# A state-space scan followed by a two-layer network on one Trainium2 core: the chunk's x tile in two halves, the first loads in another order, fewer filler matmuls and decode passes before the network starts, and eleven network cells in place of nine

## The chip, the core and the metric

The kernel runs on one core of a Trainium2 (trn2) chip. The metric is the device time of one execution, in microseconds (us); lower is better. Engines are named as in the profile: PE is TensorE, with PEld its weight loads, DVE is VectorE, ACT is ScalarE, POOL is GpSimd, and SP is the queue from which nearly all DMA transfers are issued.

## The reference

A scan with a decaying state runs per batch and head, and a two-layer network with a leaky ReLU runs on its result. The shapes are 4 batches, 8 heads, 768 positions, head width 32 and state width 16; the network has width 256, inner width 2048, and 3072 tokens.

```python
for c in range(nc):                                    # chunks of a sequence
    cum = np.cumsum(la, axis=-1)                       # la = log(clip(a))
    L = np.exp(cum[:, :, :, None] - cum[:, :, None, :]) * causal
    CB = np.einsum('bhin,bhjn->bhij', Cc, Bc)
    y_intra = np.einsum('bhij,bhjd->bhid', CB * L, xc)
    y_inter = np.einsum('bhin,bhnd->bhid', Cc, state) * np.exp(cum)[:, :, :, None]
    y[:, :, sl] = y_intra + y_inter
    Bx = np.einsum('bhjn,bhjd->bhjnd', Bc, xc) * np.exp(cum[:, :, -1:] - cum)[..., None, None]
    state = np.exp(np.sum(la, axis=-1))[:, :, None, None] * state + np.sum(Bx, axis=2)
...
h = x @ w_in                                           # x: y of all heads, 3072 x 256
g = np.maximum(0.01 * h, h)
return (g @ w_out).astype(np.float32)
```

The two weight matrices arrive as 64-bit floats, the rest as 32-bit floats.

## The kernel before

**The scan.** The kernel cuts the sequence into 8 chunks of 96 positions. One *unit* u is one chunk c of one batch b (u = 4c + b), so there are 32 units of 96 tokens. For a unit, PE computes the scores of its heads into PSUM tiles `sc` (`scores`, L288) and the exponents of its decay into a PSUM tile `pd` (`decay_pe`, L234); ACT takes the exponential into `lt` (L242); DVE multiplies the scores into `lt` (L293, two instructions a unit). PE then multiplies `lt` with the chunk's x tile `xs` (`unit_products`, L305), and `xs` with `bn` for the state that goes to the next chunk (L314). ACT copies that state to `stage` (L336), POOL copies it from there into the last 16 rows of the next chunk's `xs` (L339, four instructions a unit), ACT rounds the result to `xh` (L341), and DVE stores what the rounding lost in `xl` (L344). The names `bc`, `bn` and `xs` are the inputs of a chunk, loaded by `fetch_bc`, `fetch_bn` and `fetch_x`. POOL multiplies the decay into `bn` (`state_decay`, L269).

**The lead-in.** Units 0 to 15 run before the network, in one loop (L579 and after). Iteration u issues `scores(u + 1)`, the products of unit u, the decay of unit u + 2, then `xl` of unit u, and then some weight-decode passes. The second argument of `scores` is a number of dummy matmuls of a zero tile (`keep_warm`, L104) that PE runs first: two for u = 0 and 1, and one for every later u, 17 in all. `score_tile` has two buffers and `free_tile` (`pd`) has two, so the products of unit u + 1 may start only when `xh` and `xl` of unit u have been read out of their tile.

**The weights.** The inner width is cut into 16 blocks f of 128. The 64-bit weights of a block (`raw`, `fetch_w`) are turned into a 32-bit value and then into two rounded halves, `wh` and `wl`. It takes an `Abs` on ACT (`decode_abs`, L390) and, in this order on DVE, the passes hold (L395), shift (L401), rest of block f - 1 (L428, which makes `wl`), sign (L408) and low (L415), and a cast on ACT between low and rest (`decode_high`, L421, which makes `wh`). `decode(n)` runs the next n DVE passes. The lead-in runs 17 of the 79; the table `PASSES` gives how many follow in each step of the network.

**The network.** The 3072 tokens form six tiles t of 512. One *step* is a pair (t, f): `ffn_in` issues six matmuls of 128 x 128 by 512 columns into `hp` (L486; in each half of the input the order is `xh` by `wh`, `xh` by `wl`, `xl` by `wh`), ACT makes `gh` (L493) and the activated `hp` (L496), DVE makes `gl` (L499), and three steps later `ffn_out` issues six matmuls into the accumulators `op` (L510). The table `CELLS` gives the order of the steps: a cell (t, lo, hi) is tile t with the blocks lo to hi - 1. At the end of a cell the accumulators are copied out or added to what an earlier cell of the tile left (L527, L531, L533). Units 16 to 31 run in pairs within the network, after the steps in the table `PAIR` (`pair_block`).

**What sets the order.** Each engine runs its instructions in the order in which this code issues them; nothing reorders them afterwards. SP's queue is issued in that order too. In the lead-in's code the first loads are: `la`, `bc` and `xs` of chunk 0; then, after the split sums, `parts_d`, `bn` of chunk 0, weight block 0, the rows `dr` and `dl` for the decay of units 2 to 5 (`decay_rows_of`), `bc`, `bn` and `xs` of chunk 1, block 1 and `xs` of chunk 2.

## Time and profile before

| | |
|---|---|
| median of the runs | 327.06 us (327.05 to 327.64, 3 runs) |
| the profiled execution | 326.36 us, of which the traced span is 324.7 us |
| PE busy over the span | 316.9 us (98%), 2439 matmuls |
| DVE, ACT, POOL busy | 160.3, 167.4 and 80.5 us |
| DMA moved | 27.86 MB, 86 GB/s on average |
| first matmul of the network | 40.76 us after the span's start |

A row of a timeline gives the start in us from the span's start, the duration in us, the engine, the line, the operation, the tile written and the tiles read, the shapes, and how many like instructions were merged into the row (x2). In brackets stand the idle time of the engine before it and what ended that. The word "issue" means that the engine waited for nothing that the profile shows. A DMA row on SPq is the time of issuing, not of the transfer. Busy times of PE overlap, since matmuls are pipelined: starts tell more than durations there.

### The profile page before, as it was taken

The page shows a single profiled execution, that of the slowest core. Times are in us where ns is not written, and L with a number is a line of the kernel's source. Part 1 is how long each engine was busy: PE and PEld are TensorE (multiplying, and loading weights), DVE is VectorE, ACT ScalarE, POOL GpSimd, SP SyncE. Part 2 cuts the span into 40 slices and gives each one's busy share as a digit, 9 for nine tenths or more (in the row PEclk, how much of TensorE's full clock was granted, in tenths as well). Part 3 has the DMA queues.
Part 4 walks back from the last instruction along what each step waited for, and adds up shares of the span by engine and source line. Part 5 has one row for each costly group of instructions (what it writes and reads, how often), then busy time and mean ns, then how long its engine had stood idle before and what let it go on. Part 6 is the DMA issues. An engine that isn't in the chain of part 4 may idle for free.

```text
span 324.7 us, 6255 instructions
## 1 busy us (share of the span) xinstructions
PE 316.9 (98%) x2439; PEld 250.4 (77%) x2440; DVE 160.3 (49%) x305; ACT 167.4 (52%) x334; POOL 80.5 (25%) x164
## 2 busy tenths in 40 slices
PE   8889999999999999999999999999999999999995
PEld 4456587888788877887788888888878788888883
DVE  5679978967688543524434342525252312322221
ACT  5567776674756545353454545453544444444431
POOL 3667820000010243454034543434210000000000
PEclk9999999999999999999999999999999999999999
DMA  5998032342891001602311090202010000100001
GB/s 159 311 312 249 30 118 73 129 131 78 281 297 32 1 0 67 203 9 74 107 23 65 0 280 27 87 2 86 2 65 2 0 0 2 63 3 0 3 0 65
DMA packets 10616, 27.86 MB, mean 86 GB/s; under 512 B 2170, under 2 KB 2650, under 8 KB 10586
## 3 DMA queue, kind: packets, MB, share of 16 engines
q1 hardware_dynamic: 10442, 27.33, 26.9%
q8 instruction: 19, 0.31, 0.4%
q10 hardware_dynamic: 144, 0.13, 0.1%
q14 instruction: 11, 0.09, 0.1%
HBM read 24.14 MB, written 3.32 MB: 85 GB/s over the span
## 4 chain that ended last, share of the span: by engine, by line
PE 95%; DMA 2%; DVE 1%; issue 1%; ACT 0%; SPq 0%; ACTq 0%
PE op L510 41%; PE hp L486 39%; PE sc L288 2%; PE pd L305 2%; PE sc L365 2%; PE sc L305 2%; PE pd L234 2%; PE sc L104 1%; DMA dl<-parts_d 1%; PE sc L486 1%; PE pd L314 1%; DMA parts_d<-parts 0%; PE sc L314 0%; PE pd L208 0%; DVE lt L293 0%
## 5 line engine op out<-in xcount | busy, mean ns | idle before, releaser
L499 DVE TENSOR_TENSOR gl<-hp,gh 128x512 fp32r<-128x512 f32 x94 | 65.0, 691 | 143.7 <-ACT hp L496 143.3
L493 ACT ACTIVATE gh<-hp 128x512 fp32r<-128x512 f32 x94 | 56.1, 597 | 110.6 <-PE hp L486 110.6
L510 PE MATMUL op<-gh,wh 128*128 128x512 f32 x192 | 76.3, 397 | 0.0
L510 PE MATMUL op<-gh,wl 128*128 128x512 f32 x192 | 74.8, 390 | 0.0
L510 PE MATMUL op<-gl,wh 128*128 128x512 f32 x192 | 74.8, 389 | 0.0
L486 PE MATMUL hp<-xh,wh 128*128 128x512 f32 x188 | 73.3, 390 | 0.0
L486 PE MATMUL hp<-xl,wh 128*128 128x512 f32 x188 | 73.2, 389 | 0.0
L486 PE MATMUL hp<-xh,wl 128*128 128x512 f32 x188 | 73.1, 389 | 0.0
L496 ACT ACTIVATE hp<-hp 128x512 f32<-128x512 f32 x94 | 55.7, 593 | 0.0
L510 PEld LDWEIGHTS op<-gh,wh 128*128 128x128 f32 x192 | 36.0, 188 | 10.5 <-issue 2.3
L510 PEld LDWEIGHTS op<-gl,wh 128*128 128x128 f32 x192 | 36.0, 188 | 7.6
L510 PEld LDWEIGHTS op<-gh,wl 128*128 128x128 f32 x192 | 36.1, 188 | 7.1
L339 POOL COPY xs<-stage 16x64 f32<-16x64 f32 x112 | 31.3, 280 | 39.7 <-ACT stage L336 29.6
L486 PEld LDWEIGHTS hp<-xh,wl 128*128 128x128 f32 x188 | 35.3, 188 | 7.4
L486 PEld LDWEIGHTS hp<-xh,wh 128*128 128x128 f32 x188 | 35.3, 188 | 7.4
L486 PEld LDWEIGHTS hp<-xl,wh 128*128 128x128 f32 x188 | 35.3, 188 | 7.3
L254 POOL TENSOR_TENSOR lt<-lt,ccol 112x768 f32<-112x768 f32 x16 | 23.5, 1469 | 50.5 <-DMA lt<-crow_d 49.4
L263 POOL TENSOR_SCALAR_AFFINE_SELECT lt<-lt 96x768 f32<-96x768 f32 x16 | 14.0, 875 | 59.5 <-ACT lt L262 59.5
L293 DVE TENSOR_TENSOR lt<-sc,lt 112x384 f32<-112x384 f32 x32 | 16.3, 549 | 3.1 <-ACT lt L242 1.9
L374 DVE TENSOR_TENSOR lt<-sc,lt 112x384 f32<-112x384 f32 x32 | 15.6, 549 | 0.5
L262 ACT ACTIVATE lt<-lt 112x768 f32<-112x768 f32 x16 | 13.4, 839 | 4.1 <-POOL lt L254 4.1
L242 ACT ACTIVATE lt<-pd 112x768 f32<-112x768 f32 x16 | 13.1, 816 | 2.1 <-PE pd L215 2.1
(89 smaller groups left out, 242.4 us busy)
## 6 DMA issues: line engine op xcount, KB each, us to landing
raw<-w_l SPq DMA_DIRECT2D x16, 512.0 KB, 3.4
lt<-crow_d SPq DMA_DIRECT2D x16, 336.0 KB, 4.7
bc<-bc_l SPq DMA_DIRECT2D x8, 608.0 KB, 5.8
xs<-x_l SPq DMA_DIRECT2D x8, 384.0 KB, 9.4
out_l<-ob SPq DMA_DIRECT2D x11, 256.0 KB, 2.8
bn<-bn_l SPq DMA_DIRECT2D x8, 231.0 KB, 5.7
out_l<-obh ACTq DMA_DIRECT2D x1, 128.0 KB
out_l<-obh SPq DMA_DIRECT2D x1, 128.0 KB, 1.8
```

The lines of the kernel that those rows point to most:

```text
L242: nc.scalar.activation(lt.rearrange("p (g h) i -> p g (h i)", g=2), space[:QE, :, :4 * Q], AF.Exp)
L254: nc.gpsimd.tensor_tensor(out=lts[u], in0=lts[u], in1=ccol[:, u * NH:(u + 1) * NH].unsqueeze(2).to_broadcast([QE, NH, Q]), op=ALU.subtract,)
L262: nc.scalar.activation(lt, lt, AF.Exp)
L263: nc.gpsimd.affine_select(out=lt[:Q], in_=lt[:Q], pattern=[[0, NH], [1, Q]], compare_op=ALU.is_ge, fill=0.0, base=0, channel_multiplier=-1,)
L293: nc.vector.tensor_tensor(out=heads, in0=sc[:QE, :, :2 * Q], in1=heads, op=ALU.mult)
L339: nc.gpsimd.tensor_copy(to[:, :, hh], stage[hh * D:hh * D + N])
L374: nc.vector.tensor_tensor(out=heads, in0=spaces[half][:QE, :, 2 * Q * e:2 * Q * (e + 1)], in1=heads, op=ALU.mult,)
L486: nc.tensor.matmul(hp, lhsT=w_half[half][:, f, k * 128:(k + 1) * 128], rhs=x[t][:, k, :], start=(n == 0), stop=(n == 5),)
L493: nc.scalar.activation(ghs[s], hp, AF.Prelu, alpha=0.01)
L496: nc.scalar.activation(hps[s], hps[s], AF.Prelu, alpha=0.01)
L499: nc.vector.tensor_tensor(out=gls[s], in0=hps.pop(s), in1=ghs[s], op=ALU.subtract)
L510: nc.tensor.matmul(op, lhsT=w_half[half][:, f, DM + m * 128:DM + (m + 1) * 128], rhs=x, start=(first and i == 0), stop=(last and i == 2),)
```

## The change

The x tile of a chunk becomes two tiles of two batches each, loaded by two transfers of 2 KB a row. `bn` of chunk 0 is loaded right behind the x of chunk 0, weight block 0 behind `bc` of chunk 1, and x of chunk 1 ahead of `bn` of chunk 1. The lead-in runs one dummy for u = 2 and 3 and none from u = 4 on (6 in all), and 12 decode passes, with the first two of them and the first `Abs` one unit later. `CELLS` has eleven cells, with tiles 0, 1 and 2 visited in turn, and `PASSES` and `PAIR` change with it.

```diff
 CELLS = (
-    (0, 0, 3), (1, 0, 6), (2, 0, 6), (0, 3, 16), (1, 6, 16), (2, 6, 16), (3, 0, 16), (4, 0, 16),
-    (5, 0, 16),
+    (0, 0, 2), (1, 0, 4), (2, 0, 6), (0, 2, 10), (1, 4, 12), (2, 6, 16), (0, 10, 16), (1, 12, 16),
+    (3, 0, 16), (4, 0, 16), (5, 0, 16),
...
-PAIR = {16: 28, 18: 33, 20: 38, 22: 45, 24: 51, 26: 56, 28: 61, 30: 68}
+PAIR = {16: 29, 18: 34, 20: 38, 22: 44, 24: 51, 26: 56, 28: 61, 30: 68}
...
-PASSES = (1, 1, 2, 2, 4, 1, 4, 4, 3, 3, 3, 0, 3, 3, 3, 3, 2, 0) + (3,) * 7
+PASSES = (2, 2, 2, 4, 1, 2, 2, 2, 1, 3, 2, 3, 3, 3, 1, 3, 3, 2) + (3, 3, 3, 3, 0) + (3,) * 6
...
     def alloc_x(c):
-        xss[c] = pxs.tile([QE, NB, DM], F32, name="xs")
+        for g in range(2):
+            xss[c, g] = pxs.tile([QE, NB // 2, DM], F32, name="xs")
...
     fetch_x(0)
+    fetch_bn(0)
...
         nc.sync.dma_start(parts_d, parts)
-        fetch_bn(0)
-        fetch_w(0)
         decay_rows_of(DIRECT, SLOTS)
         fetch_bc(1)
+        fetch_w(0)
+        fetch_x(1)
         fetch_bn(1)
-        fetch_x(1)
         fetch_w(1)
...
-        decode_abs(0)
         for u in range(PE_DECAY):
             if u + 1 < PE_DECAY:
-                scores(u + 1, 2 if u < 2 else 1)
+                scores(u + 1, (2, 2, 1, 1)[u] if u < 4 else 0)
...
-            if u == 0:
+            if u == 1:
+                decode_abs(0)
                 decode(2)
-            elif u != 3:
+            elif u in (2, 3) or u % 2:
                 decode(1)
-            if u == 2:
+            if u == 1:
                 state_decay(1)
...
         settle()
-        decode(1)
+        decode(2)
```

How the order moves is shown at three places. Line numbers of the changed kernel are 6 or 7 higher. The first place is SP's queue from the x of chunk 0 to the x of chunk 2, before:

```order
L96 DMA xs<-x_l 96x1024
L561 DMA parts_d<-parts 128x288
L90 DMA bn<-bn_l 112x528
L82 DMA raw<-w_l 128x1024
L224 DMA dr<-parts_d 3x32x96
L227 DMA dl<-parts_d 24x4x96
L86 DMA bc<-bc_l 128x1216
L90 DMA bn<-bn_l 112x528
L96 DMA xs<-x_l 96x1024
L82 DMA raw<-w_l 128x1024
L96 DMA xs<-x_l 96x1024
```

and now:

```order
L100 DMA xs<-x_l 96x512 x2
L90 DMA bn<-bn_l 112x528
L568 DMA parts_d<-parts 128x288
L231 DMA dr<-parts_d 3x32x96
L234 DMA dl<-parts_d 24x4x96
L86 DMA bc<-bc_l 128x1216
L82 DMA raw<-w_l 128x1024
L100 DMA xs<-x_l 96x512 x2
L90 DMA bn<-bn_l 112x528
L82 DMA raw<-w_l 128x1024
L100 DMA xs<-x_l 96x512 x2
```

The first `bn` and the first `raw` no longer stand between `parts_d` and the `dr` and `dl` that are read from it.

The second place is DVE in the lead-in, from `xl` of unit 0 over the multiply of unit 2 (the first L293) to that of unit 3 (`w_202` before and `w_292` now are weight block 0), before:

```order
L344 TENSOR_TENSOR xl<-pd,xh 128x2x96
L395 TENSOR_SCALAR w_202<-w_202 128x512
L401 TENSOR_SCALAR w_202<-w_202 128x512
L293 TENSOR_TENSOR lt<-sc,lt 112x384 x2
L344 TENSOR_TENSOR xl<-pd,xh 128x2x96
L408 SCALAR_TENSOR_TENSOR w_202<-raw,w_202 128x512
L293 TENSOR_TENSOR lt<-sc,lt 112x384 x2
```

and now:

```order
L351 TENSOR_TENSOR xl<-pd,xh 128x2x96
L300 TENSOR_TENSOR lt<-sc,lt 112x384 x2
L351 TENSOR_TENSOR xl<-pd,xh 128x2x96
L402 TENSOR_SCALAR w_292<-w_292 128x512
L408 TENSOR_SCALAR w_292<-w_292 128x512
L300 TENSOR_TENSOR lt<-sc,lt 112x384 x2
L351 TENSOR_TENSOR xl<-pd,xh 128x2x96
```

Hold and shift of block 0 now stand between `xl` of unit 1 and the multiply of unit 3; their `Abs` stands on ACT behind the exponential of unit 3.

The third place is DVE where the network starts, from the last multiply of the lead-in to the second `gl` (before, `w_813` is block 3 and `w_600` block 2; now `w_764` is block 2 and `w_380` block 1), before:

```order
L293 TENSOR_TENSOR lt<-sc,lt 112x384 x2
L344 TENSOR_TENSOR xl<-pd,xh 128x2x96
L395 TENSOR_SCALAR w_813<-w_813 128x512
L344 TENSOR_TENSOR xl<-pd,xh 128x2x96
L401 TENSOR_SCALAR w_813<-w_813 128x512
L428 TENSOR_TENSOR wl<-w_600,wh 128x512
L499 TENSOR_TENSOR gl<-hp,gh 128x512
L408 SCALAR_TENSOR_TENSOR w_813<-raw,w_813 128x512
L499 TENSOR_TENSOR gl<-hp,gh 128x512
```

and now:

```order
L300 TENSOR_TENSOR lt<-sc,lt 112x384 x2
L351 TENSOR_TENSOR xl<-pd,xh 128x2x96 x2
L402 TENSOR_SCALAR w_764<-w_764 128x512
L408 TENSOR_SCALAR w_764<-w_764 128x512
L435 TENSOR_TENSOR wl<-w_380,wh 128x512
L506 TENSOR_TENSOR gl<-hp,gh 128x512
L415 SCALAR_TENSOR_TENSOR w_764<-raw,w_764 128x512
L422 SCALAR_TENSOR_TENSOR w_764<-raw,w_764 128x512
L506 TENSOR_TENSOR gl<-hp,gh 128x512
```

The last `wl` that DVE makes ahead of the first `gl` was that of block 2 and is now that of block 1, and the pass ahead of the last `xl` is now behind it.

More of the change, by code (lines that the diff above doesn't have):

```diff
@@ L63, in scan_ffn @@
     pbc = ctx.enter_context(tc.tile_pool(name="pbc", bufs=2))
-    pxs = ctx.enter_context(tc.tile_pool(name="pxs", bufs=3))
+    pxs = ctx.enter_context(tc.tile_pool(name="pxs", bufs=6))
     plt = ctx.enter_context(tc.tile_pool(name="plt", bufs=4))
@@ L92, in alloc_x @@
     def alloc_x(c):
-        xss[c] = pxs.tile([QE, NB, DM], F32, name="xs")
+        for g in range(2):
+            xss[c, g] = pxs.tile([QE, NB // 2, DM], F32, name="xs")
     def fetch_x(c, eng=nc.sync):
-        eng.dma_start(xss[c][:Q].rearrange("p b c -> p (b c)"), x_l[c])
+        for g in range(2):
+            n = NB // 2 * DM
+            eng.dma_start(
+                xss[c, g][:Q].rearrange("p b c -> p (b c)"), x_l[c][:, g * n:(g + 1) * n]
+            )
     idle = const.tile([128, 512], BF16, name="idle")
@@ L300, in unit_products @@
         kk = QE if c else Q
-        mt, xs = lts[u], xss[c][:, b]
+        mt, xs = lts[u], xss[c, b // 2][:, b % 2]
         for g in range(2):
@@ L336, in unit_halves @@
             nc.scalar.copy(stage, space[:, :, off + Q:off + Q + D])
-            to = xss[c + 1][Q:QE, b].rearrange("n (g h d) -> n g h d", g=2, d=D)
+            to = xss[c + 1, b // 2][Q:QE, b % 2].rearrange("n (g h d) -> n g h d", g=2, d=D)
             for hh in range(4):
```

## Prediction

> **What bounds the kernel now.** I read the page first: its span, PE's busy share and the granted clock.
>
> ```profile
> span 324.7 us, 6255 instructions
> PE 316.9 (98%) x2439; PEld 250.4 (77%) x2440; DVE 160.3 (49%) x305; ACT 167.4 (52%) x334; POOL 80.5 (25%) x164
> PEclk9999999999999999999999999999999999999999
> ```
>
> 98% hides two different stages. A view by windows shows the network's start:
>
> ```profile
> 40.00:56.00 16.00, 15.99 (x98) 12.82 (x99) 12.84 (x25) 11.43 (x24) 2.58 (x8) 1.00 0.29 99
> ```
>
> PE is busy for 15.99 of 16 us: in the network PE is the bound, and no edit here removes any of its 1152 matmuls. Time can be won only ahead of the first network matmul (T), and lost wherever PE comes to wait. In the lead-in I read the timeline of unit 8, a plain one:
>
> ```profile
> 27.17 0.36 DVE L344 TENSOR_TENSOR xl<-pd,xh 128x192 fp32r<-128x192 f32 x1 [0.18 <-ACT xh L341]
> 27.45 0.68 DVE L408 SCALAR_TENSOR_TENSOR w<-raw,w 128x512 uint32<-128x512 uint32 x1
> 27.71 0.32 PEld L305 LDWEIGHTS pd<-lt,xs 112*32 112x32 f32 x16 [0.24 <-DVE xl L344]
> 28.04 1.01 DVE L293 TENSOR_TENSOR lt<-sc,lt 112x384 f32<-112x384 f32 x2
> 28.31 0.53 PE L234 MATMUL pd<-dr,dl 123*112 123x384 bf16 x2
> 28.53 0.21 ACT L336 COPY stage<-pd 128x64 f32<-128x64 f32 x1 [0.64 <-POOL xs L339]
> 28.68 0.38 PE L104 MATMUL sc<-idle 128*128 128x512 bf16 x1
> 28.99 0.71 PE L288 MATMUL sc<-bc 32*112 32x192 f32 x8
> 29.00 0.36 DVE L344 TENSOR_TENSOR xl<-pd,xh 128x192 fp32r<-128x192 f32 x1
> 29.62 0.54 PE L305 MATMUL pd<-lt,xs 112*32 112x96 f32 x16
> ...
> 21.92 0.54 PE L305 MATMUL pd<-lt,xs 112*32 112x96 f32 x16
> 38.92 0.54 PE L305 MATMUL pd<-lt,xs 112*32 112x96 f32 x16
> ```
>
> Three loops run at nearly the same pace. PE from products to products takes 29.62 - 27.71 = 1.91, of which the dummy takes 28.99 - 28.68 = 0.31. DVE from `xl` to `xl` takes 1.83 with a decode pass in it. The third goes around: products to `stage` 0.82, `stage` to `xl` 0.47, `xl` itself 0.36, and a wake-up of about 0.05 (below): 1.70. The last two rows are the products of units 5 and 14: nine units in 17.00 us, 1.89 each.
>
> **The change part by part.** *The start.* The rows of units 0 to 2, with the quiet round trip of one small transfer:
>
> ```profile
> 7.92 0.32 SPq L227 DMA_DIRECT2D dl<-parts_d  x1
> 9.59 1.06 POOL L269 TENSOR_TENSOR bn<-bn,erev 112x512 f32<-112x512 f32 x1 [4.24 <-DMA bn<-bn_l]
> 10.70 0.33 PE L314 MATMUL pd<-xs,bn 96*32 96x32 f32 x16 [0.27 <-POOL bn L269]
> 11.43 0.66 ACT L390 ACTIVATE w<-raw 128x512 f32<-128x512 f32 x1 [1.57 <-DMA raw<-w_l]
> 11.70 0.53 PE L234 MATMUL pd<-dr,dl 123*112 123x384 bf16 x2 [0.66 <-DMA dl<-parts_d]
> 12.71 0.43 DVE L395 TENSOR_SCALAR w<-w 128x512 f32<-128x512 f32 x1
> 13.53 1.02 DVE L293 TENSOR_TENSOR lt<-sc,lt 112x384 f32<-112x384 f32 x2
> 14.28 0.81 ACT L242 ACTIVATE lt<-pd 112x768 f32<-112x768 f32 x1
> 15.32 1.02 DVE L293 TENSOR_TENSOR lt<-sc,lt 112x384 f32<-112x384 f32 x2
> ...
> parts_d<-parts SPq DMA_DIRECT2D x1, 72.0 KB, 1.6
> ```
>
> POOL ends at 10.65 and PE starts at 10.70: the wake-up of 0.05. With `bn` loaded early the wait of 0.27 goes. With nothing but `bc` behind it in the queue, `dl` issued at 7.92 lands by about 7.92 + 1.6 = 9.5, so the 0.66 goes too: 0.93 earlier. It is then given back. `Abs` of block 0 now stands behind the exponential of unit 3, and hold and shift behind it stand ahead of the scores of unit 3 on DVE. That exponential starts at 14.28 - 0.93 = 13.35 and ends at 14.16; `Abs` 0.66 gives 14.82; hold to the next multiply takes 13.53 - 12.71 = 0.82, so the multiply of unit 3 comes at 15.64 against 15.32. Instructions of one engine overlap a little (in unit 8 the pass at 27.45 starts 0.08 before the `xl` ahead of it has ended), and the start to start of this chain is shorter for that, so I take 0; the ends are 0.3 later and 0.9 earlier.
>
> *The stall at unit 4.* PE stops in the middle of one unit's products, with no semaphore:
>
> ```profile
> 18.77 0.44 PE L305 MATMUL pd<-lt,xs 112*32 112x96 f32 x9
> 20.29 0.37 PE L305 MATMUL pd<-lt,xs 112*32 112x96 f32 x7 [1.08 <-issue]
> ...
> q1 hardware_dynamic: 518, 1.36, 101.2%
> q8 instruction: 1, 0.02, 1.8%
> ```
>
> The last two rows are the DMA view of 17 to 21 us: all engines are full of loads, and one block of program code goes through in that stretch. I read the 1.08 us as PE waiting for code behind the loads. The loads stay the same but for one early `bn`, and by the zero above PE comes here at about the same time. The ends are 0 and 1.08 earlier; in between I take 0.5.
>
> [...]
>
> *Units 5 to 14.* Without dummies PE's loop falls to 1.60; the loop through ACT and DVE stays at 1.70; DVE's stays at 1.83 where a two-input pass is left (units 9, 11 and 13). Nine units: 6 x 1.70 + 3 x 1.83 = 15.7, so 1.3 are won. More code blocks come in this stretch, and a faster PE reaches them sooner: I take 1.2. The ends are 0 (code) and 9 x 0.29 = 2.6 (PE alone). *Edits at nothing.* The two x tiles make two DMA issues of one, some 0.4 of SP's time each; behind them in the queue stand loads for units that come 4 us and more later, and no row above waits for x. If that cover fails, a late x shows as PE waiting for DMA at unit 4. `state_decay` of chunk 1 moves ahead of unit 2's state copies on POOL; if `bn` of chunk 1 is late, those copies queue behind it, and the next to wait are units 6 and 7, four units (4 x 1.70 = 6.8 us) later.
>
> The first matmul of the network thus comes 1.7 earlier.
>
> *The network's start.* Here are the rows around T = 40.76:
>
> ```profile
> 40.76 0.50 PE L486 MATMUL hp<-xh,wh 128*128 128x512 f32 x1
> 41.48 0.36 DVE L344 TENSOR_TENSOR xl<-pd,xh 128x192 fp32r<-128x192 f32 x1 [0.56 <-ACT xh L341]
> 41.75 0.41 DVE L401 TENSOR_SCALAR w<-w 128x512 uint32<-128x512 uint32 x1
> 42.08 0.72 DVE L428 TENSOR_TENSOR wl<-w,wh 128x512 fp32r<-128x512 f32 x1
> 42.48 0.39 PE L486 MATMUL hp<-xh,wl 128*128 128x512 f32 x1
> 43.57 0.69 DVE L499 TENSOR_TENSOR gl<-hp,gh 128x512 fp32r<-128x512 f32 x1 [0.77 <-ACT hp L496]
> 43.81 0.60 ACT L493 ACTIVATE gh<-hp 128x512 fp32r<-128x512 f32 x1 [0.27 <-PE hp L486]
> 45.38 0.58 ACT L493 ACTIVATE gh<-sc 128x512 fp32r<-128x512 f32 x1
> 47.92 0.39 PE L486 MATMUL hp<-xh,wl 128*128 128x512 f32 x1
> 55.34 0.19 PEld L510 LDWEIGHTS op<-gh,wh 128*128 128x128 f32 x1 [0.43 <-DVE ob L533]
> ```
>
> Step 1 is block 1, and its second matmul (42.48, T + 1.72) needs `wl` of block 1. Before, that was made in the lead-in; now it is the third pass behind the last `xl`. That `xl` starts at T + 0.72; hold follows after 0.27, shift after 0.43 (12.71's duration), `wl` after 0.33, and it lasts 0.72: T + 2.47. PE waits 0.75 there. Step 4 is block 2. ACT starts `gh` of step 1 at T + 3.05 + 0.75 = 3.8; the six passes gh, hp, `Abs`, the cast of `wh`, gh, hp follow at (45.38 - 43.81) / 3 = 0.52 and end at about 7.0; `gl` of step 2 takes 0.69, and `wl` of block 2 ends 0.72 later, at T + 8.4. PE needs it at 47.92, T + 7.16 + 0.75 = 7.9: another 0.5. Step 5 needs block 3, whose low, hold, shift and `wl` all stand behind `gl` of step 3, which stands behind `wl` of block 2: I estimate 0.45 by the same durations, and 0.25 for the accumulator of the two-block cell, whose copy on DVE ends behind them. Sum: 1.95. The ends are 0.75 (the later ones hidden) and 3.0. Before, none of these waits is there: from 42.48 to 47.92 PE starts 24 matmuls at an even 0.227 us.
>
> *Two more cells.* The last row is such a boundary: PE's weight loads stood still for 0.43. Two more cost 0 (if other work hides them) to 0.9; I take half, 0.4. The tables `PAIR` and the later `PASSES` move work between steps in which DVE has room: a step is 12 matmuls, 12 x 0.227 = 2.72 us, and a `gl` with three passes takes at most 0.69 + 3 x 0.68 = 2.73, less the overlaps. I take 0.
>
> The sum is 1.95 + 0.4 - 1.7 = 0.65 slower. On the profiled execution of 326.36 (1.66 around its span) that gives 327.0; the median of the runs stands 0.70 above that execution, so I forecast 327.06 + 0.65 = 327.7. A measurement can tell about 0.2% (0.65 us) from no change, and this lies at that edge.
>
> **The rivals.** *The code stall goes* (faster). If PE's code comes in time and the loop through ACT and DVE is shorter than its rows add up to, the stall's 1.08 and 2.1 of the units are won: 3.2 against 2.35, or 326.2. For it: PE reports `issue`, which other traffic could decide. Against it: the loads are no fewer, and 1.70 is a sum of four rows. It decides once T comes before 37.7 (2.35 + 0.65 ahead of 40.76). *The two cancel*: T comes 2.4 earlier, or the later waits at the network's start hide: 327.1. For it: 0.9 at the start need not be given back whole. *Code binds* (slower): PE runs faster between two blocks and stops at each, so the units win 0.4 or less: 1.95 + 0.4 - 0.5 = 1.9 slower, 328.9. For it: the rows above. *The clock falls*: the dummies were what kept PE active. With half the clock the PE loop of 1.60 doubles in ten units: 10 x (3.2 - 1.89) = 13, and the time is 340. Against it: PEclk stayed at 9 through the 1.08 us stop, and PE works in every unit.
>
> [...]
>
> **How the numbers follow.** My forecast has 0.36 (its own range 327.4 to 328.6), cancelling 0.33, faster 0.18, code-bound 0.10, the clock 0.03. That makes slower 0.49, within 0.2% 0.33, faster 0.18. The range from 326.0 to 328.9 leaves out half of the faster case, half of the code-bound one and the clock.
>
> **What would show it.** The profile after should have: no wait for `bn` or `dl` at 10 to 12 us; the multiply of unit 3 near 15.3; a PE `issue` stop in or near unit 4; units 5 to 14 at about 1.75 each; T near 39.1; PE waits on DVE `wl` in steps 1, 4 and 5 of 0.75, 0.5 and 0.45. I am wrong if T comes before 38, or if step 1 does not wait.

## The result, and the profile after

The changed kernel takes 333.09 us (median of 5 runs, 332.2 to 333.81) against 327.64 (5 runs) for the kernel before: a ratio of 1.0123, 95% interval 1.0079 to 1.0166. It is slower, and by more than forecast (327.7, range 326.0 to 328.9). The profiled execution took 333.81 us against 326.36, which is 7.45 more.

The page of the changed kernel, in the lines that the prediction showed of before:

```profile
span 332.1 us, 6259 instructions
PE 321.9 (97%) x2428; PEld 252.5 (76%) x2429; DVE 163.9 (49%) x309; ACT 167.5 (50%) x334; POOL 78.1 (24%) x164
PEclk9955999999999999999999999999999999999999
```

PE's busy time is 5 us higher with 11 matmuls fewer, and the granted clock has two slices at 5. The view by windows, cut where the clock changes (columns: window, its length, busy time and count of PE, PEld, DVE, ACT and POOL, granted clock, DMA share, GB/s), the changed kernel first:

```profile
14.55:17.97 3.42, 1.32 (x25) 0.78 (x28) 2.70 (x6) 1.69 (x4) 1.02 (x1) 1.00 1.03 288
17.97:21.38 3.41, 3.41 (x70) 2.33 (x58) 3.34 (x7) 1.81 (x4) 2.63 (x9) 0.50 0.84 225
21.38:31.62 10.24, 10.24 (x152) 5.90 (x147) 5.28 (x13) 5.54 (x14) 5.01 (x17) 0.50 0.71 223
```

and the kernel before where it has its stop of 1.08 us:

```profile
18.88:22.29 3.41, 2.33 (x62) 1.42 (x64) 1.88 (x5) 2.24 (x5) 1.83 (x8) 1.00 1.05 350
```

In the changed kernel PE works for 1.32 of the 3.42 us up to 17.97 (39%), and from then to 31.62 its clock is halved. That is 13.65 us, four times 3.41. In the lead-in before, the emptiest such window had 68%, and the clock stayed. What emptied the window stands in the timeline:

```profile
8.76 0.43 SPq L82 DMA_DIRECT2D raw<-w_l  x1
14.54 0.66 ACT L397 ACTIVATE w<-raw 128x512 f32<-128x512 f32 x1 [1.11 <-DMA raw<-w_l]
15.24 0.43 DVE L402 TENSOR_SCALAR w<-w 128x512 f32<-128x512 f32 x1 [2.21 <-ACT w L397]
16.04 1.02 DVE L300 TENSOR_TENSOR lt<-sc,lt 112x384 f32<-112x384 f32 x2
16.64 0.38 PE L110 MATMUL sc<-idle 128*128 128x512 bf16 x1 [2.26 <-DVE lt L300]
16.95 1.06 POOL L276 TENSOR_TENSOR bn<-bn,erev 112x512 f32<-112x512 f32 x1 [3.42 <-DMA bn<-bn_l]
17.24 1.32 DVE L415 SCALAR_TENSOR_TENSOR w<-raw,w 128x512 uint32<-128x512 uint32 x1
```

Weight block 0 is issued at 8.76, now behind the 608 KB of `bc`, and ACT waits for it until 14.54. ACT had been free for 1.11 us by then. Hold and shift follow on DVE, only then comes the multiply of unit 3 (16.04), and PE stands for 2.26 us. Products and network, the changed kernel first (units 2, 3, 8, 14 and the first network matmul), then units 2, 3 and 8 of before:

```profile
13.26 0.54 PE L312 MATMUL pd<-lt,xs 96*32 96x96 f32 x16
17.62 0.60 PE L312 MATMUL pd<-lt,xs 96*32 96x96 f32 x16
31.49 0.57 PE L312 MATMUL pd<-lt,xs 112*32 112x96 f32 x16
42.78 0.54 PE L312 MATMUL pd<-lt,xs 112*32 112x96 f32 x16
45.87 0.50 PE L493 MATMUL hp<-xh,wh 128*128 128x512 f32 x1 [1.06 <-DVE xl L351]
```

```profile
15.11 0.54 PE L305 MATMUL pd<-lt,xs 96*32 96x96 f32 x16
16.91 0.54 PE L305 MATMUL pd<-lt,xs 96*32 96x96 f32 x16
27.72 0.53 PE L305 MATMUL pd<-lt,xs 112*32 112x96 f32 x14
```

With unit 14 (38.92) and T (40.76) of before, which the prediction shows, this splits the lead-in:

| stretch | before | after | difference |
|---|---|---|---|
| start to unit 2 | 15.11 | 13.26 | -1.85 |
| unit 2 to 3, with the stop | 1.80 | 4.36 | +2.56 |
| unit 3 to 8, at half clock after; with the 1.08 stop before | 10.81 | 13.87 | +3.06 |
| unit 8 to 14, at full clock, without dummies after | 11.20 | 11.29 | +0.09 |
| unit 14 to T, with the wait for `xl` of unit 15 | 1.84 | 3.09 | +1.25 |
| T | 40.76 | 45.87 | +5.11 |
| T to the end of the span | 283.9 | 286.2 | +2.3 |

The waits of the network's start (steps 4 and 5, and a change of accumulator):

```profile
53.71 0.50 PE L493 MATMUL hp<-xh,wl 128*128 128x512 f32 x1 [0.51 <-DVE wl L435]
56.91 0.50 PE L493 MATMUL hp<-xh,wl 128*128 128x512 f32 x1 [0.17 <-DVE wl L435]
58.63 0.40 PE L517 MATMUL op<-gl,wh 128*128 128x512 f32 x1
59.08 0.50 PE L517 MATMUL op<-gh,wh 128*128 128x512 f32 x1
```

One thing is needed to read what follows: executions of one kernel differ in how many windows of 3.41 us they lose to the half clock. One such window takes 0.005 off an execution's mean clock (3.41 x 0.5 of some 325 us; the four of the profiled changed kernel left 0.979). Of 133 runs of the kernel before made beside the experiments, 50 had a mean clock under 0.996, with a median of 329.7 us; the others have 327.06 us. The ratios leave out only runs more than 1.5% above the fastest of their kernel, so that most runs with lost windows are in them; the table counts all.

### The profile page after: what moved, and what is told of

It reads as the page before. It is cut to its first block, busy times and chain, and to the rows that moved or that the text cites. A ratio compares the mean times of both kernels' runs of the same rounds, so it can differ in the third digit from the quotient of the medians.

```text
span 332.1 us, 6259 instructions
## 1 busy us (share of the span) xinstructions
PE 321.9 (97%) x2428; PEld 252.5 (76%) x2429; DVE 163.9 (49%) x309; ACT 167.5 (50%) x334; POOL 78.1 (24%) x164
## 4 chain that ended last, share of the span: by engine, by line
PE 88%; ACT 3%; DVE 3%; DMA 2%; issue 2%; SPq 0%; ACTq 0%; DVEq 0%
PE op L517 39%; PE hp L493 37%; PE sc L295 3%; PE pd L312 2%; PE sc L372 2%; PE sc L312 2%; PE pd L241 2%; DMA raw<-w_l 2%; ACT gh L500 1%; PE sc L110 1%; PE pd L321 1%; ACT hp L503 1%; DVE w L415 1%; DMA parts_d<-parts 1%; ACT w L397 1%
## 5 line engine op out<-in xcount | busy, mean ns | idle before, releaser
L346 POOL COPY xs<-stage 16x64 f32<-16x64 f32 x112 | 28.8, 257 | 43.7 <-ACT stage L343 34.1
```

The costliest lines, as they stand in the source:

```text
L346: nc.gpsimd.tensor_copy(to[:, :, hh], stage[hh * D:hh * D + N])
```

## The experiments

Theory, from the two traces: the late block 0 made the stop, the stop halved the clock, and the missing dummies did neither harm nor good. Rival: without dummies the clock falls anyway.

| kernel | median us (runs) | clock under 0.996 | ratio to before, 95% interval | T | span - T |
|---|---|---|---|---|---|
| changed | 333.09 (5) | 5 | 1.0123, 1.0079 to 1.0166 | 45.87 | 286.2 |
| e1 changed, 17 dummies | 332.25 (10) | 9 | 1.0099, 1.0058 to 1.0140 | 44.56 | 286.2 |
| e2 changed, block 0's passes a unit later | 332.86 (4) | 4 | 1.0141, 1.0033 to 1.0249 | 44.36 | 286.2 |
| e3 both | 332.47 (4) | 4 | 1.0118, 1.0037 to 1.0199 | 44.31 | 286.3 |
| e4 before, 6 dummies | 327.85 (10) | 6 | 1.0002, 0.9958 to 1.0046 | 42.08 | 283.9 |
| e5 changed, block 0 back | 329.88 (10) | 4 | 1.0035, 0.9995 to 1.0075 | 41.40 | 286.9 |
| e6 changed, 17 passes | 332.36 (4) | 3 | 1.0130, 1.0050 to 1.0211 | 42.47 | 286.4 |
| e7 same, PSUM pools swapped | 331.04 (10) | 7 | 1.0088, 1.0046 to 1.0130 | 42.75 | 286.4 |
| e8 before, early `bn` | 327.43 (10) | 5 | 0.9987, 0.9951 to 1.0023 | 43.35 | 283.9 |
| e9 before, two loads later | 329.79 (10) | 7 | 0.9989, 0.9934 to 1.0043 | 46.70 | 283.9 |
| e10 same, early `bn` | 330.02 (10) | 9 | 1.0059, 1.0020 to 1.0099 | 41.19 | 283.9 |
| e11 before, eleven cells | 328.46 (10) | 4 | 1.0020, 0.9976 to 1.0064 | 41.68 | 284.6 |
| e12 before, x halves | 326.24 (10) | 0 | 0.9937, 0.9895 to 0.9979 | 40.40 | 283.9 |
| e13 x halves, 6 dummies | 327.32 (12) | 7 | 0.9984, 0.9946 to 1.0023 | 40.28 | 283.9 |
| e14 x halves, late block 0 | 328.44 (12) | 5 | 1.0040, 1.0005 to 1.0074 | 42.89 | 285.5 |
| e15 x halves, early `bn` | 327.18 (12) | 6 | 0.9977, 0.9944 to 1.0011 | 42.66 | 283.9 |
| e16 x and weights in halves | 328.69 (12) | 7 | 1.0005, 0.9970 to 1.0040 | 42.98 | 283.9 |
| e17 x halves again | 326.59 (12) | 3 | 0.9976, 0.9948 to 1.0004 | 41.11 | 284.0 |
| e18 x halves, x of chunk 2 later | 325.82 (12) | 1 | 0.9956, 0.9930 to 0.9983 | 43.29 | 283.9 |

T and span are of the one profiled execution, which may have lost windows where the median run did not. Executions also start differently: the first scores of unit 0 start between 6.45 and 7.98 us in the 20 traces, and at 7.32 and 7.89 in two executions of one kernel (e12 and e17). A difference of T under some 0.6 us says little for that. The span after T is 3.8 us more than the count to PE's last matmul that the expectations use.

### The stop or the dummies

e1 puts the dummies back; e2 moves Abs, hold and shift of block 0 behind the multiply of unit 3; e3 does both; e4 takes the dummies from the kernel before.

```diff
e1, e3 (e4 the reverse, on the kernel before)
-                scores(u + 1, (2, 2, 1, 1)[u] if u < 4 else 0)
+                scores(u + 1, 2 if u < 2 else 1)
e2, e3
-            if u == 1:
+            if u == 2:
                 decode_abs(0)
                 decode(2)
-            elif u in (2, 3) or u % 2:
+            elif u == 3:
+                decode(2)
+            elif u > 4 and u % 2:
                 decode(1)
```

> The changed kernel with the dummies back as before (two for u = 0 and 1, one for every later u, 17 in all); the stop of 2.3 us ahead of the multiply of unit 3 stays. In the changed kernel the granted clock is 0.5 from 17.97 to 31.62 us. Theory A (the stop alone brings the clock down): it falls again behind the stop, to 0.5 for 10 to 14 us; dummies of 0.31 us at full clock then cost 0.6 each in some four units, so T is 46 to 48 and the time 333 to 336. Theory B (it takes the stop and the missing dummies together) and theory C (the missing dummies alone): the clock stays at 1.0, the products of unit 5 come near 21.4, T near 40.7, and the time is 329.3 (between 328.5 and 330.2).

> The changed kernel with Abs, hold and shift of weight block 0 one unit later, so that they stand behind the multiply of unit 3 and its late data stops nobody; the loads are the same, 12 passes in the lead-in, 6 dummies. The stop of 2.3 us should go (multiply of unit 3 near 14.4 in place of 16.04). Theories A and B: without the stop the clock stays at 1.0, units 5 to 14 run at 1.75 each, T is 38 to 39 and the time 326 to 328. Theory C (missing dummies alone): the clock falls to 0.5 somewhere behind 18 us for 13.65 us, T is 43 or more and the time 331 or more.

> Both edits: no stop and 17 dummies. All theories: the clock stays at 1.0; units 5 to 14 run at 1.8 to 1.89 each, T is 39 to 40. The time is 327 to 329: by the prediction's sums 2.35 of the network's start and cells stay, less what the start and the code stall give. The difference from the kernel with the same edit and 6 dummies, where that keeps its clock, is the price of 11 dummies: 1.2 by the prediction, 0 if the loop through ACT and DVE sets the pace.

> The kernel before with one edit: one dummy for u = 2 and 3, none from u = 4 on. Its stop of 1.08 us at unit 4 stays or is met a little otherwise. Theories A and B: the longest stop of PE is 1.1 us, the clock stays at 1.0, nine units win 0.5 to 1.5, and the time is 325.6 to 326.6. Theory C: the clock falls to 0.5 behind 20 us, ten units at the doubled pace of PE's loop lose 5 us or more, and the time is 332 or more.

e1: the stop is 1.75 us, and the clock is 0.5 from 18.47 to 25.29 with all dummies in place. So the dummies don't hold the clock against that stop. At full clock the units then take as long with dummies as without (products of units 8 and 14 of e1):

```profile
30.19 0.54 PE L312 MATMUL pd<-lt,xs 112*32 112x96 f32 x16
41.55 0.54 PE L312 MATMUL pd<-lt,xs 112*32 112x96 f32 x16
```

That is 11.36 us for six units, against 11.29 for the same six in the changed kernel, which has no dummies there. e2 and e3 missed: the stop did not go, it moved to unit 4, and the clock fell in both. In e3 the rows are

```profile
16.64 0.43 DVE L402 TENSOR_SCALAR w<-w 128x512 f32<-128x512 f32 x1 [1.20 <-ACT w L397]
16.96 1.06 POOL L276 TENSOR_TENSOR bn<-bn,erev 112x512 f32<-112x512 f32 x1 [2.81 <-ACT xh L348]
17.10 1.20 DVE L408 TENSOR_SCALAR w<-w 128x512 uint32<-128x512 uint32 x1
18.82 0.38 PE L110 MATMUL sc<-idle 128*128 128x512 bf16 x1 [2.02 <-DVE lt L300]
```

DVE waits 1.20 for an Abs that was issued just ahead of its hold, and the shift takes 1.20 in place of 0.43 while POOL works at the same time (last section). e4 lost windows in 6 of 10 runs; its other runs have a median of 326.4. Neither of its expectations fits. It hints that missing dummies are not harmless either, but 6 of 10 against 50 of 133 for the kernel before is too little to show it.

### Block 0 back, the network's start, and the wait of T

e5 loads and decodes block 0 as before the change, without dummies from u = 4 on. e6 runs 17 passes in the lead-in, and e7 also swaps two lines.

```diff
e5
         nc.sync.dma_start(parts_d, parts)
+        fetch_w(0)
...
         fetch_bc(1)
-        fetch_w(0)
...
+        decode_abs(0)
         for u in range(PE_DECAY):
...
-            if u == 1:
-                decode_abs(0)
+            if u == 0:
                 decode(2)
-            elif u in (2, 3) or u % 2:
+            elif u in (1, 2) or (u > 4 and u % 2):
                 decode(1)
e6, e7
-            elif u in (2, 3) or u % 2:
+            elif u > 1:
                 decode(1)
...
-        decode(2)
+        decode(1)
e7
-    ps_h = ctx.enter_context(tc.tile_pool(name="ps_h", bufs=2, space=PSUM, reuse_waits="tile"))
     ps_o = ctx.enter_context(tc.tile_pool(name="ps_o", bufs=2, space=PSUM, reuse_waits="tile"))
+    ps_h = ctx.enter_context(tc.tile_pool(name="ps_h", bufs=2, space=PSUM, reuse_waits="tile"))
```

> The changed kernel with weight block 0 where it was: its load behind parts_d, its Abs ahead of the loop, hold and shift at u = 0, sign and low at u = 1 and 2; bn of chunk 0 stays early, 6 dummies, 12 passes. Theory (a stop of PE for a third or more of a 3.41 us window halves the clock for the windows after it, and the late block 0 made the stop): no stop at 14 to 17 us, the clock is 1.0 up to 18 us at least, at most one window is lost behind the code stop near 20 us as in the kernel before with 6 dummies. T is then 39.5 (38.8 to 40.2), or 1.7 more with one lost window, and the time T + 282.4 + 5.5 = 327.4 to 329.1. Rival (without dummies the clock falls whether PE stops or not): two to four windows are lost, T is 43 or more, the time 331 or more. Also: unit 14 now has the PSUM banks that the first hp takes, so T should not wait for xl of unit 15, and step 1 should wait for wl of block 1 instead (0.75).

> The changed kernel with 17 decode passes in the lead-in in place of 12 (one in every unit from u = 2 on); dummies, loads and cells as changed. From T to PE's last matmul the changed kernel takes 282.4 us and the kernel before 280.07. If the waits for wl in steps 4 and 5 (0.67 + 0.11 + 0.34 + 0.11 = 1.22 over the even pace) come from the missing passes, this falls to 281.2; the rest, 1.1, belongs to the two more cells. If they come from the cells, it stays at 282.4. T stays at 44 to 46, with the stop and the low clock of the changed kernel, and waits for xl of unit 15; the time is 330.5 to 332.

> As the one before, and the two PSUM pools of the network are allocated in the other order, so that the first hp takes the banks of unit 14's tile and not of unit 15's. Theory: the first network matmul waits for xl of unit 15 only since its tile lies in those banks; the wait of 1.06 us goes, T is 1.06 earlier than in the run before at an equal clock (43.3 with two low windows), T to the end stays at 281.2, the time is 1.0 lower than the run before. Rival: something else needs xl of unit 15 or a later wl, and the wait comes back in steps 1 to 5: T to the end grows by 0.7 to 1.0 and the time stays.

e5: no stop at 14 to 17 us, and the clock is 1.000 over the whole profiled run, without dummies from u = 4 on. That supports the theory, and it takes 3.2 us off the median of the changed kernel; 4 of the 10 runs still lost windows, about as often as the kernel before. But T is 41.40, not 39.5: the stop for code is back (with a second one of 0.60 at 26.52),

```profile
20.34 0.37 PE L312 MATMUL pd<-lt,xs 112*32 112x96 f32 x7 [1.13 <-issue]
41.40 0.50 PE L493 MATMUL hp<-xh,wh 128*128 128x512 f32 x1
```

and units 5 to 14 take no less than before. T no longer waits for `xl` of unit 15, which fits unit 14 having the banks of the first `hp` again; step 1 waits for `wl` 0.68 instead, as the prediction had it for T in time.

e6: the waits in steps 4 and 5 went, and others came: the accumulators waited 0.62 and 0.45 for their copies, and the span after T stayed at 286.4. The table `PASSES` still asked for ten passes in the first four steps, six before. e7: the wait of T went. The last products of unit 15 to T take 40.54 to 42.47 in e6 and 41.96 to 42.75 in e7, 1.14 less:

```profile
40.54 0.75 PE L312 MATMUL pd<-lt,xs 112*32 112x96 f32 x16 [0.42 <-DVE lt L300]
42.47 0.50 PE L493 MATMUL hp<-xh,wh 128*128 128x512 f32 x1 [1.06 <-DVE xl L351]
```

```profile
41.96 0.74 PE L312 MATMUL pd<-lt,xs 112*32 112x96 f32 x16 [0.41 <-DVE lt L300]
42.75 0.50 PE L493 MATMUL hp<-xh,wh 128*128 128x512 f32 x1
```

The span after T did not grow (286.4 in both), and the swap of the two pools is the only edit between them: I put the wait down to the bank in which the allocator had put unit 15. With block 0's passes back in e5 there is none either. The median is 1.3 lower, but the two intervals overlap, so the time alone doesn't show it.

### The parts of the change on the kernel before

```diff
e8, e10, e15
     fetch_x(0)
+    fetch_bn(0)
...
-        fetch_bn(0)
e9, e10
-        fetch_w(1)
-        fetch_x(2)
...
+            if u == 1:
+                fetch_w(1)
+            if u == 3:
+                fetch_x(2)
e11: CELLS and PAIR of the change, and
-PASSES = (2, 2, 2, 4, 1, 2, ...
+PASSES = (1, 1, 1, 2, 1, 2, ...
e12: alloc_x, fetch_x and pxs of the change, nothing else
```

> The kernel before with one edit: bn of chunk 0 is loaded right behind the x of chunk 0. The wait of 0.27 for bn goes and dl comes earlier. If the lead-in keeps this gain: T 40.1 in place of 40.76 (39.8 to 40.3) and the time 326.4. If the stop for code at unit 4 or the wait for dl gives it back: T 40.76 and the time 327.0. The clock is 1.0, or one or two windows low as in some runs of the kernel before. From T to PE's last matmul 280.07 as before.

> The kernel before with two loads issued later: weight block 1 at the end of iteration u = 1 (near 15 us) and x of chunk 2 at the end of u = 3 (near 18.5 us). Nothing else changes. In the kernels traced so far PE stops, with no semaphore, at its 448th or 449th instruction (half of unit 4's products), until 20.2 to 20.3 us, whether it comes there at 17.7 or at 19.2; 256 instructions later it stops again in some. Theory (the block of code for PE waits behind the loads in the DMA engines): with 0.9 MB less ahead of it the block comes 1 us or more earlier, the stop of 1.08 goes or shrinks below 0.4, T is 39.7 to 40.2 in place of 40.76, the time 325.4 to 326.4. Rival (the block is asked for late, whatever the loads): the stop ends at 20.2 as before, T and the time stay (40.76, 327.0).

> The kernel before with those two late loads and with bn of chunk 0 loaded right behind x of chunk 0. With early bn alone PE came to unit 4's products 1.5 us earlier and stood there for 2.5 us. Theory (code behind the loads): both gains stay, T is 38.7 to 39.5 and the time 324.5 to 325.7; no window of the clock is lost, since no stop is over 1 us. Rival (code asked for late): the stop is 2 us or more, a window or two of half clock follow, T is 42 to 43.5 and the time 327 to 329.

> The kernel before with the eleven cells, the changed PAIR and the changed PASSES, less the five passes that its longer lead-in has done already (PASSES starts 1, 1, 1, 2, 1). The lead-in stays: T 40.8 at full clock. From T to PE's last matmul the kernel before takes 280.07 and the changed one 282.4. If the waits for wl come from the five passes that the changed lead-in leaves out, it is 281.0 here (two more cells and nothing else: 0.9); if the cells cause them, 282.4. The time is 327.9 or 329.4 against 327.0.

> The kernel before with the x tile of a chunk in two halves, and nothing else. By the prediction the two more DMA issues cost nothing: T and the time stay (40.76 and 327.0, within 0.4). Rival: SP issues the loads behind them 0.4 us later for each x, and the transfers of half rows are less efficient, so that something in the lead-in comes later: T up to 1 us later, the time up to 328.

e8: the start's gain is there and is eaten. PE reaches unit 4's products at 17.25, 1.5 earlier than before, and stands (timeline, then its view by windows):

```profile
17.25 0.44 PE L306 MATMUL pd<-lt,xs 112*32 112x96 f32 x9
20.18 0.37 PE L306 MATMUL pd<-lt,xs 112*32 112x96 f32 x7 [2.50 <-issue]
```

```profile
17.88:21.29 3.41, 1.11 (x28) 0.67 (x28) 0.60 (x3) 1.64 (x5) 0.67 (x3) 1.00 1.01 284
21.29:24.70 3.41, 3.41 (x48) 2.05 (x51) 2.44 (x7) 1.74 (x5) 1.78 (x8) 0.50 1.06 293
```

The stop ends at 20.2, as in the kernel before (20.29), wherever it begins; and two windows at half clock follow, with all 17 dummies. In e10, where 0.9 MB of loads stand behind this point, no such stop is left and T is 41.19. The gain turned into a wait for a small transfer that now queues behind those loads:

```profile
28.88 0.53 PE L235 MATMUL pd<-dr,dl 123*112 123x384 bf16 x2 [1.35 <-DMA dl<-parts_d]
```

e9 shows the same (1.20 and 2.59 for `dl`). In both kernels PE comes to unit 4's products at 18.6 and passes them without a stop, where the stop lasted to 20.2 before. In the DMA view of 13 to 16 us one block of code goes through in e9 (`q8 instruction: 1`) and none in the kernel before, where it came at 17 to 21. So the code block does wait behind the loads here, and T's forecasts of both kernels failed on the next wait. e11: the span after T is 284.6, 0.7 over the kernel before. Two more cells, with the `PAIR` and the later `PASSES` that go with them, cost that. The other 1.6 of the change's 2.3 then belongs to the passes that it moved from the lead-in into the first steps; that is argued from a difference of two runs, and e6, which moved them back without changing `PASSES`, did not win it. e12, which I had expected to do nothing, is faster, and no run lost a window. Its stop for code is 0.73 instead of 1.08, but a second one follows, which the trace of the kernel before does not have:

```profile
19.42 0.37 PE L310 MATMUL pd<-lt,xs 112*32 112x96 f32 x8 [0.73 <-issue]
25.57 0.44 PE L310 MATMUL pd<-lt,xs 112*32 112x96 f32 x10 [0.50 <-issue]
```

### On a base that holds its clock

e13 takes the dummies from e12 (the edit of e4), e14 adds only the late block 0, e15 the early `bn`, and e16 splits each weight block's load in two. e17 is e12 once more, and e18 issues x of chunk 2 later on top of it.

```diff
e14
         fetch_bn(0)
-        fetch_w(0)
...
         fetch_bc(1)
+        fetch_w(0)
...
-        decode_abs(0)
...
-            if u == 0:
+            if u == 1:
+                decode_abs(0)
                 decode(2)
-            elif u != 3:
+            elif u > 1:
                 decode(1)
e16
-        eng.dma_start(raws[f].rearrange("p c w -> p (c w)"), w_l[f].bitcast(U32))
+        for g in range(2):
+            cols = slice(g * 2 * DM, (g + 1) * 2 * DM)
+            eng.dma_start(
+                raws[f].rearrange("p c w -> p (c w)")[:, cols], w_l[f].bitcast(U32)[:, cols]
+            )
e18, on e12
-        fetch_x(2)
...
+            if u == 1:
+                fetch_x(2)
```

> The kernel before with the x tile in two halves (whose clock stayed at 0.997 to 1.0 in all of its runs) and 6 dummies in place of 17. Theory (a stop brings the clock down, dummies or not; and the units are paced by ACT and DVE): no stop is added, the clock stays at 0.995 or above in nearly every run, the units take 1.8 to 2.0 as with the dummies, T is 40.0 to 40.5 and the time 326.2, the same within 0.3%. Rival (dummies hold the clock): runs of 0.99 and less appear, the median is 329 or more. Second rival (the prediction's step): PE's loop is shortened by the dummies, T 39.2, time 325.

> The kernel before with the x tile in two halves, all 17 dummies, and of the changed kernel only this: weight block 0 is loaded behind bc of chunk 1, its Abs, hold and shift at u = 1; 17 decode passes in all. Theory: the multiply of unit 3 waits for it on DVE, PE stops for 1.5 to 2.3 us between 14 and 18 us, and in most runs a window of 3.41 us falls under two thirds of PE's time and is followed by one or more windows at half the clock, with all dummies in place; T is 41.5 to 45, the time 327.5 to 331, the clock 0.985 to 0.995 in half of the runs or more. Rival (the stop alone does nothing while dummies are there): the clock stays at 0.997 or above, the stop costs at most its length, T 41 to 42, time 327 to 328.

> The kernel before with the x tile in two halves and bn of chunk 0 loaded right behind the x of chunk 0. If the stop for code at unit 4 ends when the code comes, whenever PE gets there, the gain of 0.5 to 1.0 at the start is eaten by a longer stop there: T 40.4 and the time 326.2, as with the halves alone, with a lost window of the clock in some runs. If with smaller transfers the code comes in time, T is 39.6 and the time 325.5.

> The kernel before with the x tile in two halves and each weight block loaded by two transfers of 2 KB a row in place of one of 4 KB. If shorter rows let the blocks of code through between the loads, the code block of unit 4 comes earlier than 16.9 us, the stop at PE's 448th instruction is under 0.5 (0.73 with the x halves alone, 1.08 before), T 39.9 and the time 325.7. Rival: the cost of issuing (0.4 us of SP for each) and twice the packets make later loads late; T 41 or more, time 327 or more.

> The kernel before with the x tile in two halves, once more and in more rounds, since it gave 326.24 us against 328.11 in its first comparison, with no half clock in ten runs, which no theory had forecast. If that holds, the ratio to the kernel before is 0.994 (0.990 to 0.998) again and the clock is 0.996 or more in nearly every run. If it was the luck of ten runs, the clock is 0.988 to 0.995 in four of ten runs, as in the kernel before, and the ratio is 0.998 to 1.001; the stop at PE's 448th instruction is then 0.7 to 1.3.

> The same, and x of chunk 2 is issued at the end of u = 1, behind the dr and dl of units 6 and 7 (near 15 us), in place of 10.8 us. Theory (the block of code for PE's 448th instruction and after it waits in the DMA engines behind the loads issued by 11 us): 0.39 MB less ahead of it brings the block 1 us earlier (by 16 us) and the stop there is under 0.4; later small transfers (dl of unit 8) come no later than before, T is 39.7 and the time 325.5, with fewer lost windows. Rival: the load then stands ahead of the next dr and dl or of the next block of code, the stop comes 3 to 8 us later in the lead-in as it did with two later loads, T is 41 or more and the time 327 or more.

e13: T is 40.28 against 40.40, so taking out eleven dummies is worth 0.1 us in these two executions, and units 8 to 14 take 11.29 against 11.20. The runs of e13 that lost no window have a median of 326.1, those of e12 and e17 326.2 and 326.4. But 7 of 12 runs lost windows, against 3 of 22 with the dummies (e12 and e17). That suggests that dummies do fill windows which a stop has thinned; with so few runs I call it likely, not shown. e14 makes the stop by itself (timeline, then its view by windows):

```profile
14.48 0.67 ACT L395 ACTIVATE w<-raw 128x512 f32<-128x512 f32 x1 [0.36 <-DMA raw<-w_l]
16.59 0.38 PE L109 MATMUL sc<-idle 128*128 128x512 bf16 x1 [1.52 <-DVE lt L298]
42.89 0.50 PE L491 MATMUL hp<-xh,wh 128*128 128x512 f32 x1 [1.06 <-DVE xl L349]
```

```profile
26.20:29.61 3.41, 2.13 (x48) 1.37 (x45) 3.41 (x8) 1.59 (x5) 3.01 (x8) 1.00 0.96 251
39.85:43.26 3.41, 1.97 (x70) 1.45 (x67) 2.85 (x8) 2.19 (x7) 2.81 (x9) 1.00 0.43 154
43.26:46.68 3.42, 3.42 (x10) 2.65 (x9) 0.55 (x2) 1.08 (x2) 0.60 (x1) 0.50 0.02 5
```

T's wait of 1.06 for `xl` is there too; I put it down to the PSUM banks, as in e6. Its median is 328.44 against 326.24 and 326.59 for the halves without it, its ratio 1.0040 against 0.9937 and 0.9976: the late block 0 costs about 2 us, the wait of T and the lost windows included. The clock fell in 5 of 12 runs, in the profiled one behind the wait of T and not behind the stop at 15 us, which straddled two windows (each with PE busy for some 75%). A window with 58% was followed by half the clock, one with 62% was not. e15 repeats e8 on this base (a stop for code of 1.60, then a lost window, T 42.66), and its best run of 324.64, 0.8 under the best of e12, is what the early `bn` may be worth when neither happens. e16 missed too: the stop for code stayed at 0.76, and `dl` came late twice (0.92 and 1.51).

e17: 0.9976, and 3 of 12 runs lost windows, so part of e12's margin was luck; the two intervals agree on 0.995 to 0.998. e18 has the lowest median, 325.82 us, 0.9956 (0.9930 to 0.9983) of the kernel before; its interval overlaps that of e17, so that it is faster than the halves alone is not shown. The stop for code is gone in its trace. Its profiled run is its slowest, with the rival's wait in it:

```profile
29.42 0.53 PE L239 MATMUL pd<-dr,dl 123*112 123x384 bf16 x2 [1.82 <-DMA dl<-parts_d]
```

Its 11 other runs kept a clock of 0.997 or more.

## Why the prediction was wrong, point by point

**The start (taken as 0, ends +0.3 and -0.9).** This is the step that failed first. The gain was larger than thought (1.85 by unit 2, of which 0.44 stands already at unit 0's first scores, 6.50 against 6.94, where executions differ anyway), and it was not merely given back: the multiply of unit 3 came at 16.04, not 15.3. My chain had `Abs` start at the end of the exponential, with its data there. I counted the instructions of the moved step and not its transfer, though the order showed it behind `bc` of chunk 1. It landed 5.8 us after its issue, near 14.5, and ACT waited 1.11 for it: this is the term that the sum lacked. The rest of the stop of 2.26 is the chain of `Abs`, hold and shift, which the sum had. The table's second row, 2.56, is the price of both.

**The clock (0.03, dismissed).** This is the step that cost most: 3.06 between units 3 and 8, net of the old stop. I argued from a stop of 1.08 us that left its window 68% full, and from PE working in every unit; nothing bounded a longer stop. Price and mechanism differ from my rival's: it gave 13 us to ten units without dummies; in fact five units behind a stop took 2.77 each. In the lead-ins of the 20 traces each of the nine full windows (counted from the rise of the clock) with 58% of PE's time or less was followed by the half clock, eight of them in kernels with all 17 dummies (e1, e3, e8, e9, e14, e15 and e18); every one with 65% or more kept it; of five between 60% and 64%, three kept it and two did not. The cause is shown as far as that: in the lead-in a stop that emptied a window to 58% or less had the half clock behind it. The share alone is not the whole rule. At the end of the span, where PE's last matmuls are those of the network, four windows with 44% to 52% kept the clock (47% in the kernel before, at 319.2 us), and there only windows with 42% or less lost it. The length of a window is that of the traces: in the changed kernel the clock is 0.50 from 17.97 to 31.62, 13.65 us or four times 3.41, and in e8 from 21.29 to 28.11, twice that. In the lead-in a window 39% busy, and in e14 one 58% busy, was enough. How long the clock stays low (one, two or four windows) I could not tie to anything, and what keeps e12 from losing windows is not shown (its stops for code, 0.73 and 0.50, add up to more than the one of 1.08 before).

**The stall at unit 4 (-0.5).** It vanished in the changed kernel, since PE came there later, and came back with 1.13 in e5. Reading it as code behind loads was right: in e8 it grew from 1.08 to 2.50 and ate the whole gain, and with loads moved behind it (e9, e10, e18) it went. PE's and PEld's records ahead of it, those of PE's sequencer counted, number 448 to 450 in each kernel that shows it, and 704 to 706 at the next one, 256 later.

**Units 5 to 14 (-1.2).** Wrong: 0. Units 8 to 14 took 11.29 without dummies and 11.20 with them, and e13 gives T -0.1. I let the dummy's 0.31 come off PE's loop, with the loop through ACT and DVE at 1.70 as the next limit. In the changed kernel the units took 1.72 to 2.04 instead, and the dummy's time turned into waiting (rows of units 11 to 13):

```profile
38.14 0.21 ACT L343 COPY stage<-pd 128x64 f32<-128x64 f32 x1 [1.00 <-PE pd L321]
40.09 0.27 PEld L295 LDWEIGHTS sc<-bc 32*112 32x112 f32 x4 [0.30 <-DVE lt L300]
41.04 1.02 DVE L300 TENSOR_TENSOR lt<-sc,lt 112x384 f32<-112x384 f32 x2 [0.28 <-ACT lt L249]
41.91 0.21 ACT L343 COPY stage<-pd 128x64 f32<-128x64 f32 x1 [0.32 <-PE pd L321]
```

In each of the units 9 to 14 the weight loads of PE's scores wait 0.28 to 0.30 for the multiply ahead of them, which reads the buffer that the scores are to fill. Three of the six multiplies wait as long for their exponential (0.28 to 0.36). My loop of products, `stage` and `xl` had neither of the two in it. ACT's own work is not the limit, though beside an `Abs` or a cast it adds up to 0.82 + 0.21 + 0.33 + 0.65 = 2.0: ACT stood idle for 0.3 to 1.0 ahead of each `stage` there, and the unit in which an `Abs` ran (at 40.89) was the quickest (1.72). Which chain through the three engines sets the pace stays open.

**Edits at nothing.** The x halves were not nothing but a gain of 0.2 to 0.6% (e17 and e12, the first with an interval that reaches 1). The moved `state_decay` was not nothing either: beside it DVE's sign pass took 1.32 in place of 0.68, right behind the stop.

**The network's start (+1.95 and +0.4).** The sum was right by luck, 2.35 against 2.3, and the parts were not. Step 1 did not wait, because T itself waited for `xl` of unit 15, a wait that no step had (1.25 in the table): the order showed tiles without their banks. In e5, where T did not wait for `xl`, step 1 waited 0.68, against 0.75 in the forecast. Steps 4 and 5 start 0.67 and 0.34 late, against 0.5 and 0.45. The two cells were priced at 0.4, and e11 has 0.7, with the changed `PAIR` and the later `PASSES` in it.

So the lead-in was forecast 1.7 earlier and came 5.1 later, and the rest matched in its sum alone.

## What to carry to other kernels

When a load moves in a queue, price the time at which it lands, and the chain behind it up to the engine that sets the pace, not only its instructions. A stop of PE of 1.5 to 2.5 us cost twice here: once by itself, and once more in windows of 3.41 us at half the clock (2.56 and 3.06 us in the changed kernel); look for stops that empty such a window, whatever made them. Before pricing filler matmuls, follow every chain that leads from one unit to the next through the other engines, with each of its instructions: where such a chain is as long as the unit, price the filler near nothing (eleven of 0.31 us were worth 0.1 us here), and look whether it is what keeps a window full (3 of 22 runs lost windows with the eleven, 7 of 12 without).

## What the runs showed of the hardware that was not expected

- The same program loses another number of clock windows from run to run: 326 to 331 us for the kernel before, at mean clocks from 1.000 down to 0.987 (two to three windows), with 50 of 133 runs under 0.996. A difference of 0.3% says little until the clocks of the runs are compared. Two runs stand outside of this and are not explained: one of the kernel before with 1772.83 us at a clock of 1.000, and one of e1 with 397.96 us at 0.756.
- POOL's multiply of `bn` and the decode passes on DVE hold each other up. A pass that starts while POOL multiplies took longer by most of the time that the two overlap: 1.20 instead of 0.43 us for the shift in e3 (overlap 0.91), 1.32 instead of 0.68 for sign in the changed kernel (0.77), 1.43 instead of 0.68 for low in e2 (0.88). In e2 a sign pass that had started ahead of POOL kept its 0.68, and POOL's multiply took 1.47 instead of 1.06. In the kernel before no such pass overlaps it by more than 0.15 us.
- x loaded in rows of 2 KB in place of 4 KB, the same bytes, went with an earlier end of the first stop for code, 19.4 to 20.0 us in e12, e13, e16 and e17 against 20.3 before (and 20.3 again in e15, with the early `bn`). It did not lessen the stops as a whole: 0.73 and 0.50 in e12, 0.70 and 1.05 in e17, 1.28 in e13, against 1.08. The same split of the weights (e16, 0.76) made no difference to it.
